# Keys and queries of the native jobs in one tile on space that w_out takes later; the limits loaded first; a shorter start of the first table

## The chip, the cores and the metric

The kernel runs on one core of one Trainium2 chip. The metric is the device time of one execution in microseconds, as the median of several runs. Where one execution was profiled, its own time stands beside its span, which is the part between the first and the last recorded instruction. The engines are named as the profile names them: PE multiplies matrices (PEld is its weight load), DVE, ACT and POOL work on tiles, SP issues DMAs.

## What is computed

The reference is attention with a local window and a few global keys, followed by a gated feed-forward part with a convolution along the sequence.

```python
B, H, S, D = 4, 8, 768, 64             # n_global 8, n_local 96
scores = q @ k.T / sqrt(D)             # per batch and head
keep   = key < n_global or 0 <= row - key < n_local
dist   = n_local for a global key outside the window, else |row - key|
scores = where(keep, scores - slope[head] * dist, -1e9)
a      = exp(scores - max); a = a / (sum(a) + 1e-9)
x      = (a @ v) laid out as (4, 768, 512)
h      = relu(x @ w_in)                # 512 -> 1024
c      = conv over 3 neighbours of the sequence with conv_w
out    = (h * sigmoid(c)) @ w_out      # 1024 -> 512
```

The limits n_global and n_local are inputs, so the table of distances and masks is built on the chip.

## The kernel before

**Work.** Attention is cut into 32 jobs: a batch, a half of the sequence (384 rows, `TB`), a pair of heads. A job has three steps of 128 rows, 96 steps in all. A step runs through the engines like this: scores on PE (`scores`, L620 for a native job, L622 and L623 for the others), the addition of the table and the maximum on DVE (`maximum`, L631, shown as CUSTOM_DVE or ISA), exponentials on ACT (L644), their sum and reciprocal on DVE (L654, L658), two normalisations on DVE, POOL or ACT (L667, L664), transposes on PE (L676, L677) and their way out of PSUM on ACT (`evict`, tile `pt`, L683). After three steps PE multiplies with the values (`pv`, L693), ACT and DVE split the result in a high and a low part (`xh` L707, `xl` L712), and PE can use it in `h` products (L725, three per block of 128, each 384 columns). The second half of the feed-forward part, `o` products, is L818.

**Native jobs.** The first nine jobs (`NATIVE`) multiply queries and keys as they are, in fp32. The others load keys and queries twice over (`rk`, `rq`), ACT or POOL casts them (`kk`, `qh`; L356), and DVE subtracts to get the low part (`split_k`, L360; `split_q`). Before the change the native jobs use the same buffers as these, `rk` and `kk` for keys, `qh` and `ql` for queries, with three loads for a job: keys of a whole pair of heads and two halves of queries. So `rk` of job 9 cannot be loaded before the native jobs are through with it.

**Weights.** w_in and w_out are 64-bit numbers and come in 16 pieces of 512 columns: a load `wr` (SP, L545), then ACT (`weight_top`, L552), DVE (`weight_bits`, L557), a cast on POOL (`weight_high`, L562) and a subtraction on DVE (`weight_low`, L568). Eight pieces make w_in, eight w_out.

**The table.** DVE computes `num` from the limits `nn` (L426), then `edge` (L431), which ACT needs for two operations on `off` (`beyond`, L457 and L458). The operation on the last eight columns of `off` (L461, in `middle`) waits for these two and stands in DVE's queue ahead of the first maximum.

**Order.** A planner (`Plan`) puts every instruction of the main part in order on each engine when the kernel is built. It has a cost, a due time and a list of needs for each, and times at which the engines are taken to start (`started`). Each engine works through its own list strictly as it stands. Where the planner sees PE waiting in the first 40 us it puts fillers (`warm`, L382), small products that nobody reads. SP issues nearly all loads in one queue.

Of the kernel before, what the change touches and what calls it, by code (L numbers as in the profile page):

```python
# [10 lines left out]
F32 = mybir.dt.float32  # L11
# [20 lines left out]
W0 = P  # L32
# [12 lines left out]
QROW = (0, 1, 2, 3, 0, 1, 2, 3, 2)  # L45
HK = 1024
# [232 lines left out]
WAIT = {"PE": 0, "ACT": 0, "DVE": 0, "POOL": 0, "SP": 0}  # L279
GAIN = {"PE": 0, "ACT": 0, "DVE": 0, "POOL": 0, "SP": 0}  # L280
LOADS = ("ldk", "ldq", "ldv", "wl", "lcw", "cl", "out")
# [12 lines left out]
def fast_path(tc, io):  # L294
# [24 lines left out]
    def zero_q(m):  # L319
        t = raw[m, "q"] = p2.tile([P, 2 * TB], F32, tag="qh" if m % 2 else "ql", name=f"rq{m}")  # L320
        G.memset(t[:D, TB:], 0.0)
        G.memset(t[D:, :TB], 0.0)

    def load_k(m):
        b, u, hp = jobs[m]
        w = NKC[u]
        if m < NATIVE:
            if m % 2 == 0:
                X, tag = (p2, "kk") if m // 2 % 3 else (p1, "rk")
                raw["pair"] = X.tile([P, HK], F32, tag=tag, name=f"rk{m}")  # L330
            c = m % 2 * (HK // 2)
            t = raw[m, "k"] = raw["pair"][:, c : c + w]
            nc.sync.dma_start(t, io["kn%d" % u][b, hp])
        else:
            t = raw[m, "k"] = p1.tile([P, 2 * w], F32, tag="rk", name=f"rk{m}")
            nc.sync.dma_start(t, io["qk%d" % u][b, hp][:, 2 * TB :])

    def load_q(m, j):
        b, u, hp = jobs[m]
        if m < NATIVE:  # L340
            r = slice(D * j, D * j + D)
            E = nc.sync if m + j else nc.scalar
            t = raw[m, "q"] = raw[QROW[m], "q"]
            E.dma_start(t[r, j * TB : j * TB + TB], io["qn"][b, hp, r, u * TB : u * TB + TB])
        else:
            t = raw[m, "q"] = p1.tile([P, 2 * TB], F32, tag="rq", name=f"rq{m}")
            nc.sync.dma_start(t, io["qk%d" % u][b, hp][:, : 2 * TB])
# [28 lines left out]
    nc.scalar.dma_start(nn, io["nn"].bitcast(I32).partition_broadcast(P))  # L376
# [40 lines left out]
    lt = pg.tile([P, NT], F32, tag="gh", name="lt")  # L417
# [5 lines left out]
    V.scalar_tensor_tensor(rel[:, gW], lt[:, gW], FAR, rel[:, gW], ALU.mult, ALU.add)  # L423
    nv = nn.rearrange("p (a b) -> p a b", a=2)
# [5 lines left out]
    edge = const.tile([P, 2], F32, name="edge")  # L430
    V.tensor_scalar(edge, wrap, nl, None, ALU.subtract)  # L431
# [78 lines left out]
    wih = const.tile([P, NK, FF], F32R, name="wih")  # L510
    wil = const.tile([P, NK, FF], F32R, name="wil")
    woh = const.tile([P, NF, DM], F32R, name="woh")
    wol = const.tile([P, NF, DM], F32R, name="wol")
# [10 lines left out]
    def weight_planes(i):  # L524
        if i < NK:
            h, l = wih[:, i], wil[:, i]
        else:
            j = i - NK
            h = woh[:, 2 * j : 2 * j + 2].rearrange("p f d -> p (f d)")
            l = wol[:, 2 * j : 2 * j + 2].rearrange("p f d -> p (f d)")  # L530
        return (x.rearrange("p (f n) -> p f n", f=NF) for x in (h, l))

    wraw, wt = {}, {}

    HW = HF * P

# [22 lines left out]
    def weight_high(i, half):  # L559
        t = wt[i, half]  # L560
        h, l = weight_planes(i)
        G.tensor_copy(h[:, half * HF : (half + 1) * HF], t)  # L562

    def weight_low(i, half, eng="DVE"):
        t = wt[i, half]
        h, l = weight_planes(i)
# [42 lines left out]
    def scores(s, j):  # L609
# [9 lines left out]
        if m < NATIVE:  # L619
            T.matmul(o, raw[m, "q"][:, qs], raw[m, "k"][:, k0 : k0 + n], start=True, stop=True)  # L620
            return
# [671 lines left out]
```

## Time and profile before

| what | value |
|---|---|
| median of three runs | 417.99 us (417.34 to 418.04) |
| the profiled execution | 416.73 us, its span 414.9 us |
| PE busy | 406.1 us, 98% of the span |
| DVE busy | 354.0 us, 85% |
| ACT busy | 321.2 us, 77% |
| POOL busy | 102.7 us, 25% |
| granted clock of PE | 0.998 of full speed |

The profiled execution has 1.83 us outside the span and lies 1.26 us below the median. A busy engine is one that has an instruction under way; these are means over the whole span, and the stretches differ: the first 40 us hold the loads of the weights and the first jobs, then PE hardly pauses.

### The profile page before, as it was taken

How to read it: one execution, taken by the hardware profiler on the slowest of the kernel's cores; microseconds unless marked ns; L12 is line 12 of the kernel's file. 1: busy time of each engine (PE TensorE's matmuls, PEld its weight loads, DVE VectorE, ACT ScalarE, POOL GpSimd, SP SyncE). 2: the span in 40 equal slices, each digit the busy share in tenths (PEclk: the TensorE clock that was granted, in tenths of full speed). 3: DMA queues.
4: the chain of work that ended last, by engine and by line, in shares of the span. 5: the costliest groups of instructions: out<-in, count | busy, mean ns of one | idle time of the engine just before them, and what ended most of it. 6: DMA issues, size and time to landing. Idle time of an engine off the chain costs nothing.

```text
span 414.9 us, 8589 instructions
## 1 busy us (share of the span) xinstructions
PE 406.1 (98%) x2895; PEld 365.6 (88%) x2895; DVE 354.0 (85%) x1039; ACT 321.2 (77%) x832; POOL 102.7 (25%) x161
## 2 busy tenths in 40 slices
PE   8899999999999999999999999999999999999996
PEld 7778998998899878999899888999899988898885
DVE  7989999999999999899998888699998986586700
ACT  5988999997899878798889876599788966276301
POOL 7322444643301412231223100042223200001000
PEclk9999999999999999999999999999999999999999
DMA  7999644443441334435351334534343154990111
GB/s 218 307 347 315 221 114 131 154 143 108 162 143 40 116 128 153 132 89 163 115 169 33 115 132 131 150 114 124 106 157 89 51 153 127 291 342 28 51 52 56
DMA packets 22513, 59.85 MB, mean 144 GB/s; under 512 B 2880, under 2 KB 5440, under 8 KB 22464
## 3 DMA queue, kind: packets, MB, share of 16 engines
q1 hardware_dynamic: 21952, 58.89, 44.5%
q8 instruction: 24, 0.39, 0.4%
q10 hardware_dynamic: 512, 0.36, 0.3%
q14 instruction: 25, 0.20, 0.2%
HBM read 52.95 MB, written 6.29 MB: 143 GB/s over the span
## 4 chain that ended last, share of the span: by engine, by line
PE 64%; DVE 15%; ACT 10%; DMA 6%; issue 2%; SPq 1%; ACTq 0%; DVEq 0%
PE o L818 26%; PE h L725 20%; PE pv L693 5%; DMA wr<-in_w 4%; PE t L677 3%; ACT pbuf L644 3%; PE s L623 3%; PE s L622 3%; DVE s L631 3%; PE t L676 2%; DVE c L758 2%; DVE kk L360 2%; DVE gl L808 2%; ACT pt L683 1%; PE e L846 1%
## 5 line engine op out<-in xcount | busy, mean ns | idle before, releaser
L725 PE MATMUL h<-xh,wih 128*128 128x384 f32 x256 | 92.1, 360 | 0.0
L644 ACT ACTIVATE pbuf<-s,mm 128x232 f32<-128x232 f32 (+1 forms) x192 | 83.2, 445 | 11.2 <-DVE mm L631 10.1
L725 PE MATMUL h<-xh,wil 128*128 128x384 f32 x256 | 86.4, 337 | 0.0
L725 PE MATMUL h<-xl,wih 128*128 128x384 f32 x256 | 86.3, 337 | 0.0
L758 DVE SCALAR_TENSOR_TENSOR c<-hbuf,cw,c 128x382 f32<-128x382 f32 (+1 forms) x128 | 79.1, 640 | 3.9 <-POOL c L756 3.3
L631 DVE CUSTOM_DVE_ANT_0 s<-s,tab 128x232 f32<-128x232 f32 (+1 forms) x192 | 73.0, 381 | 4.8 <-PE s L623 2.9
L818 PE MATMUL o<-woh,gh 128*128 128x512 f32 x184 | 74.9, 407 | 0.0
L818 PE MATMUL o<-woh,gl 128*128 128x512 f32 x184 | 72.7, 395 | 0.0
L818 PE MATMUL o<-wol,gh 128*128 128x512 f32 x184 | 72.6, 395 | 0.0
L683 ACT ACTIVATE pt<-t 128x464 f32<-128x464 f32 (+1 forms) x96 | 51.4, 535 | 10.4 <-PE t L677 9.6
L667 POOL TENSOR_SCALAR pbuf<-pbuf,mm 128x232 f32<-128x232 f32 (+1 forms) x44 | 32.3, 734 | 96.2 <-DVE mm L658 63.9
L725 PEld LDWEIGHTS h<-xh,wih 128*128 128x128 f32 x256 | 48.3, 189 | 0.2
L725 PEld LDWEIGHTS h<-xl,wih 128*128 128x128 f32 x256 | 48.3, 189 | 0.2
L725 PEld LDWEIGHTS h<-xh,wil 128*128 128x128 f32 x256 | 48.0, 188 | 0.0
L756 POOL TENSOR_SCALAR c<-hbuf,cw 128x382 f32<-128x382 f32 (+1 forms) x34 | 25.4, 752 | 89.5 <-ACT hbuf L733 80.4
L677 PE MATMUL t<-eye,pbuf 128*128 128x128 f32 x192 | 45.3, 276 | 0.1
L667 DVE TENSOR_SCALAR pbuf<-pbuf,mm 128x232 f32<-128x232 f32 (+1 forms) x115 | 42.5, 390 | 1.1
L818 PEld LDWEIGHTS o<-woh,gl 128*128 128x128 f32 x184 | 34.6, 188 | 8.2
L693 PEld LDWEIGHTS pv<-pt,v 128*64 128x64 f32 (+1 forms) x704 | 35.9, 136 | 6.3 <-issue 4.2
L644 ACT ACTIVATION_READ_ACCUMULATOR pbuf<-s,mm 128x1 f32 x192 | 40.4, 210 | 0.0
L693 PE MATMUL pv<-pt,v 128*64 128x128 f32 (+1 forms) x704 | 39.9, 266 | 0.5 <-ACT pt L683 0.5
L818 PEld LDWEIGHTS o<-woh,gh 128*128 128x128 f32 x184 | 34.7, 189 | 5.6
(116 smaller groups left out, 816.0 us busy)
## 6 DMA issues: line engine op xcount, KB each, us to landing
v<-in_vv SPq DMA_DIRECT2D x32, 384.0 KB, 3.7
rq<-in_qk SPq DMA_DIRECT2D x23, 384.0 KB, 3.6
check<-in_w SPq DMA_DIRECT2D x16, 512.0 KB, 4.1
wr<-in_w SPq DMA_DIRECT2D x16, 511.6 KB, 6.3
rk<-in_qk SPq DMA_DIRECT2D x12, 504.0 KB, 3.9
out<-ob SPq DMA_DIRECT2D x23, 256.0 KB, 2.2
rk<-in_qk SPq DMA_DIRECT2D x11, 400.0 KB, 3.3
rq<-in_qn SPq DMA_DIRECT2D x17, 96.0 KB, 5.6
```

The costliest lines, as they stand in the source:

```text
L622: T.matmul(o, qk[m, "h"][:, qs], qk[m, "k"][:, ks], start=True, stop=False)
L623: T.matmul(o, qk[m, "l"][:, qs], qk[m, "k"][:, ks], start=False, stop=True)
L631: V.tensor_tensor_reduce(out=o, in0=o, in1=tab[:, h, WIN:] if first else tab[:, h, 0:WIN], scale=-0.125, scalar=3.0e38, op0=ALU.add, op1=A ...
L644: last_exp[s] = A.activation(weights_of(s, j), st_s[s][:, j, :n], AF.Exp, bias=mm[:, j : j + 1], scale=-1.0, accum_out=mm[:, 2 + 2 * j : 3 ...
L667: X.tensor_scalar(x, x, y, 1.0, ALU.mult, ALU.mult)
L677: T.transpose(pt[:, c : c + P], pb[:, c : c + P], turned)
L683: A.activation(sb[:, :, :n], pt[:, :, :n], AF.Copy)
L693: T.matmul(pv[m][64 * j : 64 * j + 64, i * P + q : (i + 1) * P], vt[m][:n, i, c, 64 * j : 64 * j + 64], sb[:n, j, c * P : c * P + P - q], ...
L725: T.matmul(ps[:, :TB], w_[:, k, f * P : (f + 1) * P], x_, start=part == 0 and k == 0, stop=part == 2 and k == NK - 1,)
L756: G.tensor_scalar(c, h, x, 1.0, ALU.mult, ALU.mult)
L758: V.scalar_tensor_tensor(c, h, x, c, ALU.mult, ALU.add)
L818: T.matmul(ps, g_[:, f], w_[:, f], start=f == 0 and part == 0, stop=f == NF - 1 and part == 2,)
```

## The change

Keys and queries of a native job go to one of four tiles (`slots`, 1160 columns), whose space is that of the planes 2 to 7 of w_out (`plane`). The upper 64 partitions hold the first head and the lower 64 the second, each half in one load (`na`, `nb`): two loads for a job in place of three. The planes that lie there are written only after the last scores of the last job that used the slot (`lent`). The native jobs no longer hold `rk`, `kk`, `qh` and `ql`.

The limits `nn` move from ACT's first DMA to SP's first. In the table, two scaled copies of `rel` (`part`) are made before `num`, so that `table_w` is an operation on eight columns and one on 128; `wide` does later what the first table did before; `edge` stands behind two operations on `off`. Some of the planner's numbers change too.

```diff
-    nc.scalar.dma_start(nn, io["nn"].bitcast(I32).partition_broadcast(P))
+    nc.sync.dma_start(nn, io["nn"].bitcast(I32).partition_broadcast(P))
...
+    wof = [const.tile([P, 2, DM], F32R, name=f"wo{t}") for t in range(2)]
+    slots = [p1.tile([P, 3 * DM], F32, tag=f"wo{x}", name=f"slot{x}")[:, :NAT] for x in range(4)]
...
+    def load_n(m, j):
+        b, u, hp = jobs[m]
+        t = slots[SLOT[m]]
+        raw[m, "k"] = t[:, TB + KW - NKC[u] : TB + KW]
+        raw[m, "q"] = [t[:, TB + KW :], t[:, :TB]]
+        E = nc.sync if m + j else nc.scalar
+        if j == 0:
+            E.dma_start(t[:D, TB + KW - NKC[u] :], io["na%d" % u][b, hp])
+        else:
+            E.dma_start(t[D:, : TB + KW], io["nb%d" % u][b, hp])
...
+    for h in range(2):
+        V.tensor_scalar(part[h], rel[:, W], -(2.0 ** (2 - h)), 1.0, ALU.mult, ALU.mult)
...
-    edge = const.tile([P, 2], F32, name="edge")
-    V.tensor_scalar(edge, wrap, nl, None, ALU.subtract)
...
+    def table_w(h):
+        x = -(2.0 ** (2 - h))
+        V.tensor_scalar(part[h][:, :NGLOB], rel[:, gW], nl, x, ALU.min, ALU.mult)
+        V.scalar_tensor_tensor(tab[:, h, W], off[:, W], x * FAR, part[h], ALU.mult, ALU.add)
+
+    def wide():
+        V.tensor_scalar(rel[:, gW], rel[:, gW], nl, None, ALU.min)
+        masked(W)
+
     outside(W)
-    V.tensor_scalar(rel[:, gW], rel[:, gW], nl, None, ALU.min)
     V.scalar_tensor_tensor(off[:, gW], keyf, ng, off[:, gW], ALU.is_ge, ALU.min)
-    masked(W)
-    table(0, W)
-
+    edge = const.tile([P, 2], F32, name="edge")
+    V.tensor_scalar(edge, wrap, nl, None, ALU.subtract)
+    table_w(0)
...
+    def lent(p, t):
...
+        f = 2 * (p[0] - NK) + p[1]
+        x = 2 * t + (f - 2) // 3
+        return [("s", NB * m + NB - 1, 1) for m in range(NATIVE) if f >= 2 and SLOT[m] == x and x not in SLOT[m + 1 :]]
...
-    started = dict(PE=5000.0, ACT=1200.0, DVE=5200.0, POOL=7000.0, SP=700.0, DMA=1500.0)
...
+    started = dict(PE=4000.0, ACT=750.0, DVE=4500.0, POOL=7000.0, SP=1200.0, DMA=1800.0)
```

**DVE, from the limits to the first maximum.** Before, the list reads like this (`num` are the limits as numbers, `setup` holds `rel`, ISA is the maximum):

```order
L426 SCALAR_TENSOR_TENSOR num<-nn 128x2
L431 TENSOR_SCALAR edge<-wrap,num 128x2
L443 SCALAR_TENSOR_TENSOR off<-setup,num,lt 128x128
L449 TENSOR_SCALAR setup<-setup,num 128x8
L450 SCALAR_TENSOR_TENSOR off<-keyf,num,off 128x8
L446 SCALAR_TENSOR_TENSOR setup<-off,setup 128x128
L440 TENSOR_SCALAR tab<-setup 128x128
L454 TENSOR_SCALAR setup<-keyf,num 128x8
L461 TENSOR_SCALAR off<-keyf,num 128x8
L446 SCALAR_TENSOR_TENSOR setup<-off,setup 128x232
L631 ISA s_217,mm_185<-s_217,tab 128x128
```

With the change there is this in its place; the line numbers are those of the changed kernel:

```order
L436 TENSOR_SCALAR lt<-setup 128x128 x2
L439 SCALAR_TENSOR_TENSOR num<-nn 128x2
L454 SCALAR_TENSOR_TENSOR off<-setup,num,lt 128x128
L469 SCALAR_TENSOR_TENSOR off<-keyf,num,off 128x8
L471 TENSOR_SCALAR edge<-wrap,num 128x2
L461 TENSOR_SCALAR lt<-setup,num 128x8
L462 SCALAR_TENSOR_TENSOR tab<-off,lt 128x128
L473 TENSOR_SCALAR setup<-keyf,num 128x8
L480 TENSOR_SCALAR off<-keyf,num 128x8
L457 SCALAR_TENSOR_TENSOR setup<-off,setup 128x232
L638 ISA s_213,mm_188<-s_213,tab 128x128
```

`edge` has moved from directly behind `num` to behind two operations on `off`, the mask of 128 columns has left this stretch, and two scaled copies (into `lt`) stand ahead of `num`. The operation on eight columns of `off` that waits for ACT (L480, before L461) is still two places ahead of the first maximum.

**POOL, after the tables.** Before, POOL casts pieces of weights (`wih`) with normalisations (`pbuf`) between them:

```order
L562 CAST wih<-w_0_380 128x512
L562 CAST wih<-w_0_387 128x512
L667 TENSOR_SCALAR pbuf_182<-pbuf_182,mm_185 128x128
L562 CAST wih<-w_0_422 128x512
L562 CAST wih<-w_0_468 128x512
L667 TENSOR_SCALAR pbuf_182<-pbuf_182,mm_188 128x128
L562 CAST wih<-w_1_531 128x512
L562 CAST wih<-w_1_541 128x512
```

With the change the key cast of job 9 (`kk`) comes as the third of these:

```order
L570 CAST wih<-w_0_396 128x512
L674 TENSOR_SCALAR pbuf_185<-pbuf_185,mm_188 128x128
L366 CAST kk_463<-rk_340 128x800
L570 CAST wih<-w_0_443 128x512
L674 TENSOR_SCALAR pbuf_186<-pbuf_186,mm_189 128x232
L674 TENSOR_SCALAR pbuf_187<-pbuf_187,mm_190 128x232
L570 CAST wih<-w_0_505 128x512
L570 CAST wih<-w_0_534 128x512
```

A second key cast, that of job 10, follows this piece directly. Behind the first one stand the cast of the second weight piece and two normalisations, of steps 7 and 8.

**DVE, around the second `xl`.** Before, three operations on weight pieces lie near it:

```order
L654 TENSOR_REDUCE mm_186<-mm_186 128x2
L557 SCALAR_TENSOR_TENSOR w_0_422<-wr_0_276,w_0_422 128x512
L658 RECIPROCAL mm_186<-mm_186 128x2
L557 SCALAR_TENSOR_TENSOR w_0_468<-wr_0_347,w_0_468 128x512
L667 TENSOR_SCALAR pbuf_183<-pbuf_183,mm_186 128x232
L712 TENSOR_TENSOR xl_502<-pv_454,xh_490 128x384
L654 TENSOR_REDUCE mm_187<-mm_187 128x2
L631 ISA s_477,mm_188<-s_477,tab 128x128
```

With the change the first key split follows `xl` and a reciprocal (`mm`):

```order
L661 TENSOR_REDUCE mm_189<-mm_189 128x2
L638 ISA s_434,mm_190<-s_434,tab 128x232
L638 ISA mm_190 128x1
L719 TENSOR_TENSOR xl_484<-pv_446,xh_472 128x384
L665 RECIPROCAL mm_189<-mm_189 128x2
L370 TENSOR_TENSOR kk_463<-rk_340,kk_463 64x800
L574 TENSOR_TENSOR wil<-w_0_443,wih 128x512
L638 ISA s_498,mm_191<-s_498,tab 128x128
L638 ISA mm_191 128x1
```

The split has come in ahead of the subtraction for the second weight piece, which is the row behind it, and of the maxima of step 9. Of the weight pieces' operations DVE has fewer up to here. A second key split stands ahead of the third `xl`; before, the first key split stands behind the subtraction of the ninth weight piece.

On SP the key load of job 9 is the nineteenth DMA with the change, behind the loads of jobs 0 to 5, two loads of values and four weight pieces. On ACT a piece's `weight_top` comes some steps later in the list than before: the first four stand behind the evictions of steps 3 and 5, exponentials of step 8 and those of step 9, where before the first two stand behind the exponentials of step 5, the others behind the eviction of step 4 and the exponentials of step 7. On PE the program has 114 fillers in place of 85, of which 36 stand at the very start in both. Ahead of the transposes of step 14 stand nine `h` products fewer than before.

## Rows read from the trace of the kernel before

**Rows 1.** Busy time by stretch; columns as in its first line.
```profile
core 0: us, PE busy (x) PEld busy (x) DVE busy (x) ACT busy (x) POOL busy (x), PEclk, DMA share, GB/s
5.00:40.00 35.00, 32.57 (x278) 28.29 (x279) 32.99 (x145) 28.98 (x95) 11.94 (x25) 1.00 0.98 322
75.00:400.00 325.00, 324.45 (x2238) 292.42 (x2237) 283.96 (x761) 254.25 (x638) 70.46 (x86) 1.00 0.40 126
```

**Rows 2.** Waits of PE from 5 to 40 us: total, times, longest.
```profile
PE t L676 <- ACT pt L683: 1.2, 3, 0.8
PE pv L693 <- ACT pt L683: 0.5, 1, 0.5
PE s L620 <- ACT pbuf L644: 0.4, 1, 0.4
```

**Rows 3.** Waits of ACT in the same stretch.
```profile
ACT w L552 <- DMA wr<-in_w: 3.0, 4, 1.1
```

**Rows 4.** Waits of DVE in the same stretch.
```profile
DVE w L557 <- ACT w L552: 0.4, 1, 0.4
DVE xl L712 <- ACT xh L707: 0.3, 1, 0.3
```

**Rows 5.** Timeline of DVE, 2.5 to 6.5 us: start, duration, instruction, idle before.
```profile
2.52 0.41 DVE L419 TENSOR_SCALAR lt<-setup 128x128 f32<-128x128 f32 x1
...
3.77 0.16 DVE L426 SCALAR_TENSOR_TENSOR num<-nn 128x2 f32<-128x2 int32 x1 [0.64 <-DMA nn<-in_nn]
3.96 0.23 DVE L431 TENSOR_SCALAR edge<-wrap,num 128x2 f32<-128x2 f32 x1
4.10 0.35 DVE L443 SCALAR_TENSOR_TENSOR off<-setup,num,lt 128x128 f32<-128x128 f32 x1
...
4.88 0.29 DVE L446 SCALAR_TENSOR_TENSOR setup<-off,setup 128x128 f32<-128x128 f32 x1
...
5.48 0.38 DVE L461 TENSOR_SCALAR off<-keyf,num 128x8 f32<-128x8 f32 x1
...
6.22 0.29 DVE L631 CUSTOM_DVE_ANT_0 s<-s,tab 128x128 f32<-128x128 f32 x1
```

**Rows 6.** Timeline of ACT: the second of the two operations on `off`.
```profile
4.75 0.49 ACT L458 ACTIVATE off<-off,edge 128x232 f32<-128x232 f32 x1
```

**Rows 7.** Timeline of SP: a load of values, which ends a run of issues.
```profile
5.34 0.58 SPq L352 DMA_DIRECT2D v<-in_vv  x1
```

**Rows 8.** Busy time and rate of the DMA engines, 21.5 to 27.1 us.
```profile
21.50:27.10 5.60, 5.19 (x34) 4.72 (x34) 4.91 (x21) 4.61 (x15) 1.28 (x2) 1.00 0.98 330
```

**Rows 9.** Timeline of ACT: a weight piece taken up as it lands.
```profile
21.48 0.78 ACT L552 ACTIVATE w<-wr,misc 128x512 uint32<-128x512 fp8e4 x1 [0.90 <-DMA wr<-in_w]
```

**Rows 10.** Timeline of POOL: a key cast.
```profile
66.88 0.85 POOL L356 CAST kk<-rk 128x800 fp32r<-128x800 f32 x1 [0.66 <-DMA rk<-in_qk]
```

**Rows 11.** Timeline of DVE around the second `xl`.
```profile
21.12 0.68 DVE L557 SCALAR_TENSOR_TENSOR w<-wr,w 128x512 uint32<-128x512 uint32 x1
...
23.53 0.56 DVE L712 TENSOR_TENSOR xl<-pv,xh 128x384 fp32r<-128x384 f32 x1 [0.26 <-ACT xh L707]
```

**Rows 12.** Timeline of DVE: a key split.
```profile
70.09 0.99 DVE L360 TENSOR_TENSOR kk<-rk,kk 64x800 fp32r<-64x800 f32 x1
```

**Rows 13.** Timeline of DVE: the reciprocal of step 14.
```profile
39.48 0.16 DVE L658 RECIPROCAL mm<-mm 128x2 f32<-128x2 f32 x1
```

**Rows 14.** Timeline of POOL: one of the two normalisations behind it.
```profile
40.19 0.62 POOL L667 TENSOR_SCALAR pbuf<-pbuf,mm 128x232 f32<-128x232 f32 x1 [1.75 <-PE t L677]
```

**Rows 15.** Timeline of PE: step 14's first transpose.
```profile
42.73 0.25 PE L676 MATMUL t<-eye,pbuf 104*104 104x104 f32 x1
```

**Rows 16.** Chain of waits: a run of `h` products on PE.
```profile
167.99 2.61 PE h L725 x15
```

**Rows 17.** Timeline of PE: a run of fillers.
```profile
27.26 0.61 PE L382 MATMUL h<-setup 128*128 128x128 bf16 x8
```

**Rows 18.** Timeline of PE: its two waits between 40 and 160 us.
```profile
73.19 0.38 PE L622 MATMUL s<-kk,qh 128*128 128x232 f32 x1 [0.38 <-ACT pbuf L644]
...
148.41 0.27 PE L676 MATMUL t<-eye,pbuf 104*104 104x104 f32 x1 [0.49 <-ACT pbuf L664]
```

More of the change, by code (lines that the diff above doesn't have):

```diff
@@ L278 @@
 MORE = {("t", "PE"): 0, ("pv", "PE"): 0, ("nrm", "POOL"): 78, ("nrm", "ACT"): 46, ("exp", "ACT"): 45}
-WAIT = {"PE": 0, "ACT": 0, "DVE": 0, "POOL": 0, "SP": 0}
+WAIT = {"PE": 0, "ACT": 1, "DVE": 0, "POOL": 0, "SP": 0}
 GAIN = {"PE": 0, "ACT": 0, "DVE": 0, "POOL": 0, "SP": 0}
-LOADS = ("ldk", "ldq", "ldv", "wl", "lcw", "cl", "out")
+LOADS = ("ldn", "ldk", "ldq", "ldv", "wl", "lcw", "cl", "out")
 WARMEND = 40000.0
@@ new lines, in plane, with zero_q @@
+    def plane(t, f):
+        if f < 2:
+            return wof[t][:, f]
+        g, i = divmod(f - 2, 3)
+        if (t, g) not in wog:
+            wog[t, g] = p1.tile([P, 3, DM], F32R, tag=f"wo{2 * t + g}", name=f"wo{t}{g}")
+        return wog[t, g][:, i]
+    def zero_q(x):
+        G.memset(slots[x][D:, TB + KW :], 0.0)
+        G.memset(slots[x][:D, :TB], 0.0)
+    def load_n(m, j):
[8 more added lines that the diff above has]
+            E.dma_start(t[D:, : TB + KW], io["nb%d" % u][b, hp])
@@ L415, in fast_path @@
     V.tensor_copy(keyf, keyi)
-    lt = pg.tile([P, NT], F32, tag="gh", name="lt")
+    lt = pg.tile([P, NT + 2 * W0], F32, tag="gh", name="lt")
+    part = [lt[:, NT + h * W0 :][:, :W0] for h in range(2)]
     W, M = slice(WIN, NT), slice(0, WIN)
@@ L522, in fast_path, with weight_plane @@
     zero_q(3)
[L524 to L531, printed above, removed]
+    def weight_plane(t, i, half):
+        x = (wih, wil)[t][:, i, half * HW : (half + 1) * HW] if i < NK else plane(t, 2 * (i - NK) + half)
+        return x.rearrange("p (f n) -> p f n", f=HF)
+    HW = HF * P
     wraw, wt = {}, {}
-    HW = HF * P
     def weight_words(i, half):
@@ L560, in weight_high @@
         t = wt[i, half]
-        h, l = weight_planes(i)
-        G.tensor_copy(h[:, half * HF : (half + 1) * HF], t)
+        G.tensor_copy(weight_plane(0, i, half), t)
     def weight_low(i, half, eng="DVE"):
-        t = wt[i, half]
-        h, l = weight_planes(i)
-        sl = slice(half * HF, (half + 1) * HF)
-        (V if eng == "DVE" else G).tensor_tensor(l[:, sl], t, h[:, sl].bitcast(F32), ALU.subtract)
+        h, l = (weight_plane(x, i, half) for x in range(2))
+        (V if eng == "DVE" else G).tensor_tensor(l, wt[i, half], h.bitcast(F32), ALU.subtract)
     words, seen = {}, []
@@ L619, in scores @@
         if m < NATIVE:
-            T.matmul(o, raw[m, "q"][:, qs], raw[m, "k"][:, k0 : k0 + n], start=True, stop=True)
+            q = raw[m, "q"][j][:, i * P : (i + 1) * P]
+            T.matmul(o, q, raw[m, "k"][:, k0 : k0 + n], start=True, stop=True)
             return
@@ L816, in mm2 @@
         ps = hist["o", b, t]
-        for part, (g_, w_) in enumerate(((gh, woh), (gh, wol), (gl, woh))):
+        for part, (g_, w_) in enumerate(((gh, 0), (gh, 1), (gl, 0))):
             T.matmul(
-                ps, g_[:, f], w_[:, f],
+                ps, g_[:, f], plane(w_, f),
                 start=f == 0 and part == 0, stop=f == NF - 1 and part == 2,
@@ L1145, in general @@
             decode(t[..., 0], t[..., 1], e, y)
-            h, l = weight_planes(i)
-            A.activation(h, w, AF.Copy)
-            G.tensor_tensor(l, w, h.bitcast(F32), ALU.subtract)
+            for half in range(2):
+                h, l = (weight_plane(t, i, half) for t in range(2))
+                x = w[:, half * HF : (half + 1) * HF]
+                A.activation(h, x, AF.Copy)
+                G.tensor_tensor(l, x, h.bitcast(F32), ALU.subtract)
         r0i = gp.tile([P, S], I32, tag="q", name="r0i")
```

80 lines of the change are left out of this document (31 added, 49 removed).

## The prediction

> **What bounds the kernel now.** I read the times by stretch first. From 75 us to 400 us PE is busy for 324.45 of 325 us; from 5 to 40 us it is busy for 32.57 of 35 us and runs fillers in part of that, DVE is busy for 32.99, and the DMA engines have a share of 0.98 [rows 1]. So the kernel ends when PE has done its work, plus whatever PE lost, and nearly all of the loss is made in the first 40 us. There DVE, with 2.0 us idle, sets the pace: it adds the table for every step and decodes the weights as well. Next come the waits of that stretch. PE waits 1.2 + 0.5 + 0.4 = 2.1 us for ACT [rows 2]. ACT in turn is held four times, 3.0 us in all, by a weight piece that has not landed [rows 3]; evictions and exponentials stand behind it. DVE loses 0.4 + 0.3 = 0.7 us to ACT in the same way [rows 4]. Later there are few waits: two between 40 and 160 us, of 0.38 and 0.49 us [rows 18].
>
> PE's order is fixed, so a late step is not made up by work that stands behind it. What counts is when a step's weights are ready, against how much useful work PE has in front of it.
>
> **The start.** DVE waits 0.64 us for the limits, which ends with `num` at 3.77 [rows 5]. The two scaled copies, 128 columns each like the operation of 0.41 us at 2.52 [rows 5], fit into that wait. With `nn` as SP's first DMA I put `num` at 3.6 (3.45 to 3.85). But `edge` now comes behind `num` (0.19 to the next start), `off` (0.35) and an eight-column operation: 3.6 + 0.19 + 0.38 + 0.15 = 4.3, where it was 3.96 [rows 5]. From the start of `edge` to the end of ACT's second operation there were 4.75 + 0.49 - 3.96 = 1.28 us [rows 5, 6], so ACT ends at 5.6 in place of 5.24, and the operation that waits for it, before at 5.48, starts at about 5.7. The mask of 128 columns (0.29) that left DVE's stretch buys nothing, since DVE stands waiting for ACT. The first maximum moves from 6.22 to about 6.5: **+0.3** (+0.15 to +0.55). Behind the waiting operation stand the mask of 232 columns and all maxima.
>
> **DVE's further work before step 14.** Counting the order of both up to the reciprocal of step 14: two key splits come in, 0.99 each [rows 12], +2.0; two operations on eight columns and three on the convolution's weights at about 0.15 (the spacing of the small ones in [rows 5]), +0.7; the mask of `wide` and one more table of 360 columns at about 0.3 each (0.29 for 128 columns [rows 5]), +0.6. One bits and one low operation of a weight piece go, 0.68 long [rows 11], 0.6 in pace, -1.2; three normalisations go to other engines, about -0.75. Sum **+1.4** (+1.2 to +1.7).
>
> **The holds of ACT.** With the weights taken up some steps later in ACT's list, the pieces have landed by then. DVE gets back the 0.7 us: **-0.7** (-0.7 to 0). DVE's other idle time, 2.0 - 0.7 = 1.3 us, is spread over short waits for scores and sums; an engine that runs later finds half of that done: **-0.6** (-1.0 to 0).
>
> **The keys of job 9.** They are now SP's nineteenth DMA. Up to their end the queue carries 5.91 MB: four jobs of 0.428, two of 0.455, two loads of values of 0.393, four weight pieces of 0.524 and 0.410 of keys. In before the queue's fourth weight piece ends at 21.48, where ACT takes it up [rows 9], and by the list it has 4.94 MB up to there. The next 5.6 us ran at 330 GB/s [rows 8]: 0.97 MB more take 2.9 us, which gives 24.4. Two issues fewer stand ahead of the first load of values, at 0.58 each [rows 7], so all comes up to 1.15 us sooner: 23.25. A cast on POOL takes 0.85 [rows 10], and the split can start at 24.1. When does DVE get to it? The second `xl` started at 23.53 and took about 0.5 [rows 11]. Up to there DVE has 0.8 less work (two bits operations and one low, against the copies and the eight-column ones), gets back the 0.7, and carries the +0.3: with the reciprocal it is through at 22.9. It is held **1.2 us** (0 to 2.5). All of step 9's maxima stand behind the split, and on POOL the normalisations of steps 7 and 8 behind the cast.
>
> [...]
>
> **To PE.** Sum on DVE at step 14: 0.3 + 1.4 - 0.7 - 0.6 + 1.2 = +1.6. In before the reciprocal of step 14 starts at 39.48 [rows 13] and its last normalisation ends at 40.19 + 0.62 = 40.81 [rows 14], while PE comes to the transposes at 42.73 [rows 15]: 1.9 us to spare. But PE has nine `h` products fewer ahead of them, 9 x 2.61/15 = 1.57 us [rows 16]. So 0.3 is left, and PE loses 1.6 - 0.3 = **+1.3** (-0.3 to +2.6). Step 15 has more to spare. The fillers, 29 more at 0.61/8 = 0.076 us [rows 17] or 2.2 us, stand where PE waits anyway; the loss to 40 us has room for them, so I cost them at nothing, and at up to 2.2 where PE should be on time.
>
> **Later.** The waits of 0.38 us at 73 and 0.49 us at 148 us [rows 18], with the gaps beside them, come from ACT and DVE being late in their lists, the one at 73 just as DVE does the first key splits (the split of [rows 12] starts at 70.09). Splits done early and some 2 us less of work in ACT's list up to step 24 relieve these: **-1.0** (-1.4 to 0). The planes of w_out that must wait for the slots come late: decoding them moves behind the native jobs, to where DVE is as full as before; I cost this at nothing, since PE has `h` products of the first block to do, and it is a loss of a us or more if an `o` product waits for a plane.
>
> **Sum.** +1.3 - 1.0 = +0.3: 417.0 for an execution like the profiled one (416.73). The median is 1.26 above it, so 418.3.
>
> **The rivals.** *Faster:* the keys land by 22.0, so DVE is not held. Then 0.3 + 1.4 - 0.7 - 0.6 = 0.4 on DVE, within 0.1 of what PE has to spare, and later -1.4: 416.7. For it: the first loads begin sooner and the start of the DMA queue had room. Against it: 5.91 MB by then is more than the list of before had landed. If, besides, PE's 2.1 us behind ACT [rows 2] are what paced that stretch, and not DVE, about 1 us more is given back: 415.7.
>
> *Slower:* the engines' bytes and not SP's issues set the early landings, so that the 1.15 us do not come. The keys land at 24.4, the split can start at 25.25, DVE is held 2.35 us, and with it POOL: 0.3 + 1.4 - 0.7 - 0.6 + 2.35 - 0.3 - 1.0 = +1.45, 419.4. It decides from a landing at about 23.8 on, each us later being one us. [...] Without the later gain it is 420.4.
>
> *The change does not do what it says:* the keys of job 9 and 10 come early, but the splits only trade places with the weights, step 14 keeps its spare time, and the waits at 73 and 148 return in other places. About 418.0.
>
> **How the numbers follow.** A measurement of this kernel can tell about 0.2%, 0.84 us, from no change. My forecast of 418.3 and the last rival lie within that; I give them 0.31 and 0.05. The faster rival gets 0.31, the slower 0.33, as the price of the held split is the least certain term and each of its two sides is as near. The range of 415.7 to 420.4 spans both; the forecast's own is 417.5 to 419.1.
>
> **What would show it.** In the profile after: `edge` at about 4.3 and the first maximum at 6.4 to 6.6; no wait of ACT for `wr`; a wait of POOL for the DMA `rk` near 22 to 24 us and behind it one of DVE's split for POOL of about 1 us; PE waiting for the transposes of step 13 or 14; no wait of PE at 73. The forecast is wrong if DVE's split does not wait, if PE loses over 1 us after 75 us because an `o` product waits for a plane of w_out, or if the fillers delay scores that were ready.

## The result and the profile after

The changed kernel takes 422.26 us (422.01 to 424.08, four runs), against 417.66 us for the kernel before in runs on the same chip. The ratio is 1.0125, with a 95% interval of 1.0089 to 1.0162: slower by about 4.6 us, and above the range of the prediction. (One correction to the text ahead: a slot is 384 + 504 + 384 = 1272 columns wide, not 1160.)

The profiled execution is the longest of the four, 424.08 us at a granted clock of 0.994 over its span; the other three ran at 0.999 to 1.000 and took 422.01 to 422.40. A likely cause of that difference of 1.9 us comes out below.

Busy time by stretch, in the columns of [rows 1]:

```profile
5.00:40.00 35.00, 29.08 (x246) 25.43 (x247) 28.33 (x124) 24.43 (x78) 10.60 (x23) 0.95 1.00 287
75.00:400.00 325.00, 323.57 (x2262) 291.51 (x2262) 289.36 (x783) 260.80 (x655) 76.12 (x92) 1.00 0.41 129
```

In the first stretch PE, DVE and ACT each do less than in [rows 1]: DVE 28.33 of 35 us in place of 32.99. The DMA engines are as busy as before, 1.00 to 0.98, and move less, 287 to 322 GB/s. PE's granted clock has a mean of 0.95. From 75 to 400 us PE is busy for 323.57 us, 0.9 less than before. So the loss is made early again. It is larger than the idle time says, since fillers count as busy: those behind 20 us take 2.6 us (26 of them), against 0.9 (11) before. Who waits there, from 5 to 40 us (total, times, longest), first PE, then DVE, then POOL:

```profile
PE t L683 <- POOL pbuf L674: 4.2, 1, 4.2
PE s L627 <- POOL slot L335: 1.0, 1, 1.0
PE t L683 <- ACT pt L690: 0.5, 1, 0.5
PE t L683 <- DVE pbuf L674: 0.4, 1, 0.4
```

```profile
DVE kk L370 <- POOL kk L366: 4.5, 1, 4.5
```

```profile
POOL kk L366 <- DMA rk<-in_qk: 6.4, 1, 6.4
```

These answer to [rows 2 to 4]. PE's waits for evictions have shrunk from 1.2 to 0.5 us and ACT is no longer held by `wr` at all (no such row is left), as forecast. PE's 1.0 us is the wait for its first scores, at 5.69. In place of the others stands one long wait on each engine, and they make a chain: POOL 6.4 us for the DMA of `rk`, DVE 4.5 us for POOL's `kk`, PE 4.2 us for POOL's normalisation. (POOL also waits 9.8 us for weight pieces, ahead of this and behind it.) In the order of time, from the timelines of POOL, DVE and PE:

```profile
26.09 0.85 POOL L366 CAST kk<-rk 128x800 fp32r<-128x800 f32 x1 [6.42 <-DMA rk<-in_qk]
26.89 0.62 POOL L570 CAST wih<-w 128x512 fp32r<-128x512 f32 x1
27.48 1.19 POOL L674 TENSOR_SCALAR pbuf<-pbuf,mm 128x232 f32<-128x232 f32 x1
```

```profile
22.31 0.16 DVE L665 RECIPROCAL mm<-mm 128x2 f32<-128x2 f32 x1
26.98 1.36 DVE L370 TENSOR_TENSOR kk<-rk,kk 64x800 fp32r<-64x800 f32 x1 [4.51 <-POOL kk L366]
```

```profile
23.89 0.66 PE L627 MATMUL s<-slot 128*128 128x232 f32 x2
28.73 0.42 PE L683 MATMUL t<-eye,pbuf 104*104 104x104 f32 x1 [4.18 <-POOL pbuf L674]
```

POOL has its next instruction, the key cast of job 9, in hand from 19.7 on and starts it at 26.09. Behind it in its list stand a weight piece and, at 27.48, the normalisation of step 7. DVE is through with what stands ahead of the split at 22.47 and starts it at 26.98. PE gets its transposes of step 7 at 28.73, after 4.18 us with nothing in hand. The split itself takes 1.36 us, with a cast on POOL beside it, where [rows 12] had 0.99; the normalisation that starts beside it takes 1.19, where [rows 14] had 0.62.

The start, on DVE, beside [rows 5]:

```profile
3.29 0.48 DVE L436 TENSOR_SCALAR lt<-setup 128x128 f32<-128x128 f32 x2
3.82 0.16 DVE L439 SCALAR_TENSOR_TENSOR num<-nn 128x2 f32<-128x2 int32 x1
4.02 0.35 DVE L454 SCALAR_TENSOR_TENSOR off<-setup,num,lt 128x128 f32<-128x128 f32 x1
...
4.55 0.31 DVE L471 TENSOR_SCALAR edge<-wrap,num 128x2 f32<-128x2 f32 x1
...
5.94 0.23 DVE L480 TENSOR_SCALAR off<-keyf,num 128x8 f32<-128x8 f32 x1 [0.33 <-ACT off L477]
...
6.52 0.29 DVE L638 CUSTOM_DVE_ANT_0 s<-s,tab 128x128 f32<-128x128 f32 x1
```

`num` comes at 3.82, where it was 3.77: as SP's first DMA the limits land no sooner here, at 3.80. (In a kernel without half loads, the last one below, `num` came at 3.59.) `edge` is at 4.55, the operation that waits for ACT at 5.94, and the first maximum at 6.52, 0.30 later than before.

### The profile page after: what moved, and what is told of

The parts are those of the page before. It is cut to its first block, busy times and chain, and to the rows that moved or that the text cites. A ratio compares the mean times of both kernels' runs of the same rounds, so it can differ in the third digit from the quotient of the medians.

```text
span 422.3 us, 8640 instructions
## 1 busy us (share of the span) xinstructions
PE 409.7 (97%) x2924; PEld 368.4 (87%) x2924; DVE 355.3 (84%) x1040; ACT 322.5 (76%) x834; POOL 106.0 (25%) x162
## 4 chain that ended last, share of the span: by engine, by line
PE 69%; DVE 20%; issue 4%; ACT 4%; POOL 1%; DMA 1%; DVEq 0%; POOLq 0%; ACTq 0%
PE o L825 25%; PE h L732 23%; PE pv L700 6%; DVE s L638 4%; PE t L684 3%; DVE c L765 3%; PE t L683 3%; PE s L630 3%; PE s L629 2%; PE s L627 2%; DVE pbuf L674 2%; DVE gl L815 2%; DVE kk L370 1%; PE e L853 1%; ACT pbuf L651 1%
## 5 line engine op out<-in xcount | busy, mean ns | idle before, releaser
L825 PE MATMUL o<-wo,gh 128*128 128x512 f32 x368 | 117.5, 400 | 0.0
L765 DVE SCALAR_TENSOR_TENSOR c<-hbuf,cw,c 128x382 f32<-128x382 f32 (+1 forms) x128 | 82.4, 669 | 2.7 <-POOL c L763 1.4
L825 PEld LDWEIGHTS o<-wo,gh 128*128 128x128 f32 x368 | 64.7, 189 | 10.4
L825 PE MATMUL o<-wo,gl 128*128 128x512 f32 x184 | 72.4, 394 | 0.0
L690 ACT ACTIVATE pt<-t 128x464 f32<-128x464 f32 (+1 forms) x96 | 50.4, 525 | 11.4 <-PE t L684 11.0
L674 POOL TENSOR_SCALAR pbuf<-pbuf,mm 128x232 f32<-128x232 f32 (+1 forms) x41 | 27.6, 674 | 94.9 <-DVE mm L665 45.5
L683 PE MATMUL t<-eye,pbuf 104*104 104x104 f32 x160 | 38.3, 261 | 6.5 <-POOL pbuf L674 4.2
L674 DVE TENSOR_SCALAR pbuf<-pbuf,mm 128x232 f32<-128x232 f32 (+1 forms) x111 | 40.8, 388 | 1.0
L825 PEld LDWEIGHTS o<-wo,gl 128*128 128x128 f32 x184 | 34.5, 188 | 7.9
L651 ACT ACTIVATION_READ_ACCUMULATOR pbuf<-s,mm 128x1 f32 x192 | 38.2, 199 | 0.0
```

Source lines behind the costliest of these rows:

```text
L651: last_exp[s] = A.activation(weights_of(s, j), st_s[s][:, j, :n], AF.Exp, bias=mm[:, j : j + 1], scale=-1.0, accum_out=mm[:, 2 + 2 * j : 3 ...
L674: X.tensor_scalar(x, x, y, 1.0, ALU.mult, ALU.mult)
L683: T.transpose(pt[:NLATE, c + P : c + WIN], pb[:NLATE, c + P : c + WIN], ident[:NLATE, :NLATE])
L690: A.activation(sb[:, :, :n], pt[:, :, :n], AF.Copy)
L765: V.scalar_tensor_tensor(c, h, x, c, ALU.mult, ALU.add)
L825: T.matmul(ps, g_[:, f], plane(w_, f), start=f == 0 and part == 0, stop=f == NF - 1 and part == 2,)
```

## The experiments

Two theories came out of this. **Held lists:** the cast and the split of job 9's keys stand in POOL's and DVE's lists at a place that comes up well before the keys land, and all that is behind them pays. **Slow halves:** the keys land late, later than any row of before suggests, because loads into 64 partitions move slowly. The rivals: it is just the bytes ahead in the queue; all loads and steps are late anyway and the hold only shows it; the start is what costs. All kernels are timed against the kernel before, whose median was between 416.89 and 417.66 us in the sets of runs. So the difference of two medians from different sets is open by up to 0.8 us; the ratio, with its 95% interval in brackets, is the better measure. Where a clock is named without a stretch, it is the mean over the span of a run.

### Keys over 128 partitions, order unchanged

```diff
-        if j == 0:
-            E.dma_start(t[:D, TB + KW - NKC[u] :], io["na%d" % u][b, hp])
-        else:
-            E.dma_start(t[D:, : TB + KW], io["nb%d" % u][b, hp])
+        if j:
+            nc.sync.dma_start(raw[m, "k"], io["kn%d" % u][b, hp])
+        r = slice(D * j, D * j + D)
+        E.dma_start(raw[m, "q"][j][r], io["qn%d" % u][b, hp, r])
...
```

> The changed kernel with the same order, but each native job's keys come in one load over all 128 partitions and the queries in two loads over 64, as before the change (into the new tiles). Theory 'slow halves': loads over 64 partitions with long rows move at about 240 GB/s where loads over 128 move at about 340, so job 9's keys land about 2 us sooner (24 in place of 26.0), DVE's split is held about 2.5 us in place of 4.5, and the time falls by about 2 us, to about 420.2. Rival 'too much ahead in the queue': the keys are late because of the bytes ahead of them, at whatever shape; then with one more issue per job they land at 26 or later and the time stays at 422 to 423.

The keys' cast and split in this kernel, on POOL and DVE:

```profile
24.25 0.85 POOL L366 CAST kk<-rk 128x800 fp32r<-128x800 f32 x1 [4.60 <-DMA rk<-in_qk]
```

```profile
25.14 1.36 DVE L370 TENSOR_TENSOR kk<-rk,kk 64x800 fp32r<-64x800 f32 x1 [2.69 <-POOL kk L366]
```

The keys come 1.84 us sooner (24.25 for the cast, from 26.09), with one issue more per job, and DVE is held 2.7 us in place of 4.5. That is what slow halves said and the rival did not. One trace each would not carry it, so here are all with this list of loads, by the DMA records: with halves the keys landed at 26.04, 25.87 and 26.35 us (the changed kernel and two below that have its loads), with whole keys at 24.20, 25.39 and 23.77 (this one and two below), 1.6 us sooner in the mean. The halves carry 0.11 MB more for the four jobs with a gap (0.428 MB each, against 0.401), 0.3 us at 330 GB/s, so the bytes ahead explain a small part. The rate says it too. Two stretches of the changed kernel and of this one (columns as in [rows 1]):

```profile
5.00:10.00 5.00, 4.31 (x25) 3.94 (x25) 4.37 (x25) 3.22 (x12) 2.40 (x10) 1.00 1.01 256
20.00:25.00 5.00, 4.54 (x40) 3.62 (x36) 2.44 (x10) 3.97 (x13) 0.00 (x0) 1.00 1.05 261
```

```profile
5.00:10.00 5.00, 4.65 (x25) 3.92 (x25) 4.41 (x24) 3.21 (x12) 2.40 (x10) 1.00 0.97 295
20.00:25.00 5.00, 4.52 (x40) 3.60 (x36) 2.42 (x10) 3.94 (x13) 0.75 (x1) 1.00 1.00 317
```

With halves the engines are busy for the whole stretch and move 256 and 261 GB/s; with whole keys 295 and 317. Worked out from the packets of the trace that began between 5 and 25 us, by size:

```
kernel      bytes  partitions  packets  mean us  16 engines at that pace
before       4093     128        755     0.179    366 GB/s   weights
before       3072     128        384     0.146    337 GB/s   values
before       1600     128        254     0.073    353 GB/s   keys
before       2016     128        310     0.096    337 GB/s   keys
before       1536      64        577     0.098    250 GB/s   queries
after        4093     128        526     0.198    331 GB/s   weights
after        3072     128        366     0.167    294 GB/s   values
after        3200     128        124     0.194    264 GB/s   keys of job 9
after        3552      64        439     0.236    240 GB/s   half loads
after        3136      64        134     0.222    226 GB/s   half loads
whole keys   4093     128        616     0.195    335 GB/s   weights
whole keys   1600     128        363     0.080    320 GB/s   keys
whole keys   2016     128        279     0.120    270 GB/s   keys
whole keys   1536      64        627     0.084    292 GB/s   queries
```

A half load moves at two thirds of the pace that keys and weights had before (226 to 240 GB/s, against 337 to 366). It is not the length of the rows, since the weights' are longer and faster (4093 bytes, 331 GB/s in the same kernel). But the number of partitions alone does not give the pace of a load either: beside half loads the keys of job 9, over 128 partitions, move at 264 GB/s, and with whole keys the short rows of the queries, over 64, are no slower (292) than the keys of 2016 bytes (270). What holds in every trace is the sum: in these two stretches the queue moves 250 to 262 GB/s in the four kernels with half loads of long rows and job 9's keys at this place. With whole keys and the same places it moves 295 and 317 in this kernel; the two others, below, had 303 and 338 from 20 to 25 us. The change put the native keys, which moved at 337 to 353 GB/s, into the slow kind. What makes a half load slow, no run here shows.

The time did not fall, however: 423.47 us (1.0146, 1.0114 to 1.0179), 3 us above what was expected. All four runs were at a clock of 0.992 to 0.996, where three of the changed kernel's four were at 0.999 or 1.000. That needed a run of its own.

### The same, with fillers in the hold

```diff
+        if o.key == ("t", 7, 1):
+            warm(32)
```

> The kernel with keys over 128 partitions in the order of the changed kernel, with 32 fillers ahead of the second pair of transposes of step 7, where PE is held 2.4 us. Theory 'the hold is paid twice': the granted clock falls to about 0.5 to 0.8 for 5 us behind the hold, in all four runs of that kernel (0.992 to 0.996 over the span), and that costs up to 2 us; with fillers the clock stays at 1.00 and the time falls from 423.5 to about 421.5. If the clock's fall costs nothing there, as DVE sets the pace: 423.5.

PE's clock around the hold, in the kernel without and with fillers (the clock is the third number from the end):

```profile
22.50:27.50 5.00, 2.64 (x17) 1.89 (x15) 2.33 (x5) 2.06 (x7) 2.57 (x3) 1.00 0.97 318
27.50:32.50 5.00, 5.00 (x30) 4.68 (x29) 3.85 (x19) 3.12 (x10) 1.31 (x2) 0.66 0.89 322
32.50:37.50 5.00, 4.46 (x45) 3.76 (x43) 4.90 (x15) 4.03 (x14) 1.41 (x2) 1.00 0.82 264
```

```profile
22.50:27.50 5.00, 3.80 (x44) 3.14 (x42) 1.18 (x1) 1.88 (x6) 2.06 (x3) 1.00 1.03 323
27.50:32.50 5.00, 4.24 (x33) 3.90 (x33) 4.92 (x21) 3.26 (x11) 1.83 (x3) 1.00 0.95 324
32.50:37.50 5.00, 4.29 (x41) 3.74 (x42) 4.90 (x15) 3.96 (x14) 1.41 (x2) 1.00 0.92 292
```

Without fillers the stretch from 27.5 to 32.5 us, behind the hold, ran at a mean of 0.66 (0.53 in its first half, 0.79 in its second); with 32 idle products in the hold it ran at 1.00. The time is 421.52 us, against 423.47, and the clock 0.998 to 1.000 in all five runs. By ratios it is 1.0093 (1.0059 to 1.0127) against 1.0146 (1.0114 to 1.0179). So the hold is paid twice: PE stands still, and then it works through these 5 us, busy for all of them, at a mean clock of 0.66, which by an estimate from that mean costs (1 - 0.66) x 5 = 1.7 us there. In the changed kernel this seems to fall on some executions and not on others. The profiled one had it: 0.66 in the same stretch, and 0.50 from 28.5 to 31.0 us, at 424.08 against 422.0 to 422.4; of the other three only the mean clock is known. (In the profile of the filled kernel the keys came at 25.4 and DVE was held 3.9 us, so the loads vary by a microsecond between executions.) Where the clock holds, whole keys are worth 422.2 - 421.5, about 0.7 us, which these runs do not tell from nothing.

### Cast and split later

```diff
+    for key, behind in ((("ck", 9), ("max", 11, 1)), (("sk", 9), ("max", 12, 1)), (("ldk", 10), ("sk", 9)), (("ck", 10), ("max", 16, 1)), (("sk", 10), ("max", 17, 1)), (("ldk", 11), ("sk", 10))):
+        x = next(d for d in done if d[1].key == key)
+        done.remove(x)
+        done.insert(next(i for i, d in enumerate(done) if d[1].key == behind) + 1, x)
```

> The changed kernel with all loads up to job 9's keys where they are, but the cast and the split of these keys moved behind the maxima of steps 11 and 12 on POOL and DVE, and the load, cast and split of job 10's (and the load of job 11's) moved behind accordingly. Theory 'held lists': what costs the time is that POOL and DVE stand waiting for a load with the work of steps 7 to 9 behind them; then DVE's hold of 4.5 us and PE's of 4.2 us go, and the time is 418 to 419. Rival 'everything comes later': the weights and jobs are late as well, and the hold only shows it; then PE's loss moves to other waits and the time stays above 421.

PE's waits over 0.2 us from 25 to 50 us, in the timeline:

```profile
35.48 0.27 PE L683 MATMUL t<-eye,pbuf 104*104 104x104 f32 x1 [1.10 <-DVE pbuf L674]
...
49.55 0.66 PE L627 MATMUL s<-slot 128*128 128x232 f32 x2 [1.02 <-ACT pbuf L651]
```

The hold is gone, on POOL (0.36 us are left of 6.42) and on PE; the two waits that remain in this stretch are 1.10 and 1.02 us. The time is 420.81 us (1.0091, 1.0060 to 1.0123). That is above the 418 to 419 expected. So the held list cost about 1.5 us, beside what it does to the clock (the intervals overlap), and both theories fall short: by the ratio 3.8 us are still there. A split moved by hand in a fixed order removes the wait; the rest of the order stays as it was made, for keys, weights and queries that land earlier than they do.

### Both edits

The diff of the whole keys and the one of the later cast and split together.

> Both of the edits that the runs before tried one at a time: keys of the native jobs in one load over 128 partitions, and cast and split of job 9's keys behind the maxima of steps 11 and 12. Theory 'slow halves and held lists', both costing: with the split moved, 3.5 us of loss are left over the kernel before, made between 30 and 50 us where loads are late; loads that move at the full rate take away about 2 us of that: 418.5 to 419. Rival 'one cause': the shape of the loads matters only through the keys of job 9; then nothing is gained over the 420.8 of the moved split alone.

420.03 us (1.0080, 1.0051 to 1.0109), above the 418.5 to 419 expected. That is 0.8 us below the moved split alone, with intervals that overlap, and 3 us remain. In this kernel neither the half loads of keys nor the hold is left; what is left is an order made from other landing times. The next runs change that.

### The planner told of the half loads' price

```diff
-                add(("ldn", m, j), ("SP" if m + j else "ACT", (dma(D, (TB + (KW if j else w)) * 4), 0)), (load_n, m, j), old, due=D0 - 8900 + j)
+                add(("ldn", m, j), ("SP" if m + j else "ACT", (1.6 * dma(D, (TB + (KW if j else w)) * 4), 0)), (load_n, m, j), old, due=D0 - 8900 + j)
```

> The changed kernel with the planner's price for each load over 64 partitions multiplied by 1.6, nothing else; the planner then puts the cast of job 9's keys behind one more weight piece on POOL and the split behind the maxima of step 10 on DVE, and other places follow. Theories 'slow halves' and 'held lists' together: DVE's hold falls to 2 to 3 us, and the time to about 420. If the order around the split doesn't matter: 422.

Nothing else in the program differs; the planner makes its whole order anew, with other fillers. 419.03 us (1.0035, 1.0012 to 1.0058), where 420 was expected. The split on DVE, now behind the maxima of step 10:

```profile
27.38 1.37 DVE L370 TENSOR_TENSOR kk<-rk,kk 64x800 fp32r<-64x800 f32 x1 [0.29 <-POOL kk L366]
```

It starts at 27.38, later than in the changed kernel, and is held 0.29 us in place of 4.51 (2 to 3 us were expected). The keys land at 26.06, no sooner than in the changed kernel, so it is the order that wins and not an earlier landing. This is 3.2 us of the 4.6 that the change lost, from one number: the planner prices a load by its rows and their length, which makes a half load as fast per byte as any other. How much of the 3.2 us is the split's place, and how much another place in the new order, this run does not tell.

### The planner told of three loads, keys over 128 partitions

```diff
+            add(("ldn", m, 2), ("SP", (dma(P, w * 4), 0)), (load_n, m, 2), old, due=D0 - 9000)
             for j in range(2):
-                add(("ldn", m, j), ("SP" if m + j else "ACT", (dma(D, (TB + (KW if j else w)) * 4), 0)), (load_n, m, j), old, due=D0 - 8900 + j)
+                add(("ldn", m, j), ("SP" if m + j else "ACT", (dma(D, TB * 4), 0)), (load_n, m, j), old, due=D0 - 8900 + j)
...
```

> Keys over 128 partitions again, with the planner told of three loads for a job and their prices as before the change, so that it makes its own order. Theory 'slow halves and held lists': the planner's times for these loads now fit, so the casts and splits stand where the keys have landed; no hold of DVE over 1 us, and 416 to 418.5. Rival 'early keys cost by themselves' (two splits of 1 us more on DVE before 40 us): 419 or more even then.

417.71 us (1.0017, 0.9994 to 1.0040). No loss is left that these runs can tell from none, with the new tiles, the early keys and the new start all kept; the two loads for a job are given up. The kernel with both edits by hand has loads of the same shapes, and the intervals are apart (1.0051 to 1.0109 there). On DVE the split starts at 32.04 and waits for nothing:

```profile
32.04 1.09 DVE L371 TENSOR_TENSOR kk<-rk,kk 64x800 fp32r<-64x800 f32 x1
```

### Early keys, old place

Both with the load of job 9's keys not ahead of the last native scores, once in the changed kernel and once with whole keys and the planner told.

```diff
-            add(("ldk", m), ("SP", (dma(P, w * 8), 0)), (load_k, m), alloc=(bk,), due=D0 - 9000)
+            add(("ldk", m), ("SP", (dma(P, w * 8), 0)), (load_k, m), alloc=(bk,), due=D0 - 9000, behind=[("s", NB * NATIVE - 1, 1)])
```

> The changed kernel with the load of job 9's keys not before the last scores of a native job, as before the change; halves, limits and table as changed, order by the planner. Theory 'held lists' (the early keys are the larger part): 417.5 to 419. Rival 'slow halves' as the larger part: the native jobs' loads are as slow as in the changed kernel, so weights and later jobs land late and the time stays above 420.

419.69 us (1.0068, 1.0044 to 1.0093). Taking the early keys out of the changed kernel gives back 2.6 us, and 2 us stay. The halves are still there and may be what keeps them, which this run does not show. So neither theory holds it all.

> The same kernel of three loads for a job, with the load of job 9's keys not before the last native scores. Theory 'early keys are neither good nor bad once they are in time': 417 to 418.5. Rival 'early splits cost by themselves' (1 us of DVE before 40 us for each): below 417.0, faster than with early keys. Rival 'early keys pay' by closing the waits near 73 us: 418.5 or more.

418.42 us (1.0039, 1.0019 to 1.0060), with runs from 416.92 to 421.02; five of its twelve were at a clock of 0.994 to 0.996, and these five are the ones above 419.8. Not faster without early keys, so no cost of the early splits by themselves shows once they are in time; whether they pay is inside the scatter of the clock.

### The start

```diff
     nl, ng = num[:, 0:1], num[:, 1:2]
+    edge = const.tile([P, 2], F32, name="edge")
+    V.tensor_scalar(edge, wrap, nl, None, ALU.subtract)
...
-    edge = const.tile([P, 2], F32, name="edge")
-    V.tensor_scalar(edge, wrap, nl, None, ALU.subtract)
```

> The changed kernel with edge computed directly behind num again. Theory 'held lists': the first maximum moves from 6.52 to about 6.3, but the landing of job 9's keys sets the pace later, so the time stays at 422.2 within 0.3 us. Rival 'late start': the 0.3 us at the start goes through to the end, with what the steps behind it lose, and the time falls by 0.3 to 1 us.

423.56 us (1.0135, 1.0097 to 1.0174), with two runs at 424.1 and 424.3 and clocks of 0.996 and 0.995. DVE around the first maximum:

```profile
3.85 0.16 DVE L439 SCALAR_TENSOR_TENSOR num<-nn 128x2 f32<-128x2 int32 x1
4.05 0.35 DVE L444 TENSOR_SCALAR edge<-wrap,num 128x2 f32<-128x2 f32 x1
...
5.52 0.22 DVE L480 TENSOR_SCALAR off<-keyf,num 128x8 f32<-128x8 f32 x1
5.78 0.40 DVE L459 SCALAR_TENSOR_TENSOR setup<-off,setup 128x232 f32<-128x232 f32 x1
6.51 0.30 DVE L638 CUSTOM_DVE_ANT_0 s<-s,tab 128x128 f32<-128x128 f32 x1 [0.33 <-PE s L627]
```

`edge` is 0.5 us sooner and the operation behind ACT (L480) no longer waits. But the first maximum stays at 6.51, where 6.3 was expected, since it now waits 0.33 us for scores, and PE's first scores wait 0.8 us for a half load (`nb`). One wait took the place of another, and the time did not fall. It lies 1.3 us above the 422.2 expected, for which the two runs at a lower clock are the likely reason: the other two took 422.2 and 423.0.

The same edit in the kernel with whole keys and the planner told of three loads:

> The kernel with keys over 128 partitions and the planner told of three loads, with edge directly behind num. With halves this edit moved nothing, since the first maximum then waited for scores whose half load landed late; here the first job's loads land by 5.1, so the first maximum should come at 6.3 in place of 6.5, and the time fall by 0 to 0.3 us, to about 417.5. If it falls by 1 us or more, the start is worth more than its own delay.

417.06 us (0.9999, 0.9981 to 1.0018), 0.65 us below the same kernel without the edit, with intervals that overlap; the lowest median here, and level with the kernel before. The first maximum came at 6.56, 0.26 later than expected, against 7.04 without the edit; in both the planner put a table of 232 columns ahead of it.

In that kernel, without the edit, the start taken back to that of before:

```diff
-    nc.sync.dma_start(nn, io["nn"].bitcast(I32).partition_broadcast(P))
+    nc.scalar.dma_start(nn, io["nn"].bitcast(I32).partition_broadcast(P))
...
-    table_w(0)
+    masked(W)
+    table(0, W)
...
```

> The same kernel of three loads for a job in the new tiles, with the whole start (limits on ACT's queue, table, edge) as before the change. Theory 'the start costs little': within 0.8 us of 417.7, the sign open, since DVE has about 0.5 us less to do and the limits no later. Rival 'the new start pays': 418.5 or more.

417.33 us (1.0012, 0.9996 to 1.0029), level with 417.71 and 417.06: the new start shows neither a gain nor a cost. DVE's first maximum in this kernel:

```profile
7.51 0.28 DVE L630 CUSTOM_DVE_ANT_0 s<-s,tab 128x128 f32<-128x128 f32 x1
```

It is a microsecond later than in the changed kernel (6.52), and the time is 5 us lower. So the rival that the late start is what costs is out.

And the new start alone, in the kernel before, which is the reverse of that diff:

> The kernel before with only the changed start: limits as SP's first DMA, the two scaled copies, the shorter first table, edge behind two operations on off, wide later; loads of the native jobs as before the change, the rest by the planner with its numbers of before. Theory 'the start costs little': num comes no sooner (the limits landed at 3.80 with the change, at 3.75 before), edge later, the first maximum 0.2 to 0.3 us later than 6.22, and the time within 0.8 us of the kernel before. Rival 'the start is a good part of the loss': over 418.5.

418.14 us (1.0034, 1.0014 to 1.0054). The first maximum came at 6.39, 0.17 later, where 0.2 to 0.3 was expected, and `num` at 3.59, sooner than the 3.77 of before and not as late as expected. The time is at the edge of the 0.8 us allowed, and its interval lies above no change. PE's longest wait in this kernel's first 75 us is one of 1.3 us for ACT's exponentials, in an order that the planner made anew. What the start costs alone was not told apart from that. So an order made anew may cost the better part of a microsecond by itself, which was not tried apart, and a difference of that size between two kernels with different orders is not put down to their edit.

## Why the prediction was wrong

**The step that failed** is the one on the keys of job 9: "the split can start at 24.1", DVE "held **1.2 us** (0 to 2.5)". The mechanism was right, down to the engines and the normalisations behind it; the landing was mis-sized. By the trace's DMA records the keys landed at 26.04, not at 23.25, the split started at 26.98, and DVE was held 4.5 us. The loads had been put at the pace of before, and 1.15 us taken off for two issues fewer. The pace was lower: from 15 to 25 us the changed kernel moved 271 GB/s where the one before moved 310, although its DMA engines had the higher share (1.04 and 0.92). With whole keys the keys landed 1.6 us sooner in the mean, so the halves are about that much of the 2.8, give or take the microsecond by which executions differ.

The 1.15 us came at first and did not last. The first values landed at 10.22 in place of 11.48, but the fourth weight piece at 23.43 in place of 21.46. With three loads for a job the first values landed as early (10.22 to 10.70 in three traces), so the saved issues are not shown to be what helped. SP issued the keys' load at 15.24, 10.8 us before it landed: there the engines and not SP set the landing, as the slower rival had it (24.4). That rival named the place and the sign, but its price too was made with the pace of before.

In the changed kernel the first six half loads landed one after another, 0.8 to 1.1 us apart, from 4.64 to 9.45 us. By the packets from 5 to 25 us half loads moved at 226 to 240 GB/s, where the keys before moved at 337 to 353 and the queries, half loads too, at 250.

**To PE** failed next. The hold was put into the sum at step 14, less what PE had to spare there. It was paid at step 7, at once and in full (4.18 us), because PE's list had nothing else to do ahead of those transposes; and it brought the clock down in some runs, for which there was no term at all (1.9 us where it falls). With the measured hold in place of 1.2 us and nothing for the later gain, the prediction's own sum would be 0.3 + 1.4 - 0.7 - 0.6 + 4.5 - 0.3 = +4.6, or 422.6. That this is near 422.26 is in part chance, as the path was another and the small terms were not measured.

**Later, -1.0,** did not come. The waits near 73 and 148 us are gone, as forecast, and others took their place: PE has 0.7 + 0.4 us of waits behind 45 us in the changed kernel; 40 to 75 us lost 0.4 less than before and 75 to 400 us 0.9 more. A planner that knows the price does not end these: PE's waits behind 40 us add up to 3.7 us with the price alone and to 3.0 with whole keys. What those kernels win they win early, where PE is idle for 1.9 and 1.6 us from 5 to 40 us in place of 5.9.

**What held.** The first maximum: +0.30, forecast +0.3. In part that is luck, since `num` was at 3.82 and not at 3.6, `edge` at 4.55 in place of 4.3 and the operation that waits for ACT at 5.94 in place of 5.7, and from there to the maximum it took 0.58 us and not the 0.74 of before. ACT's holds by `wr`: gone. The planes of w_out in the slots: no `o` product waits for a plane in the list of waits. The fillers, put at nothing: the kernel with whole keys and the planner told has more of them behind 20 us (30, 2.2 us) and no loss, so their number is not what costs. The small terms on DVE (+1.4, -0.7, -0.6) were not measured one by one; the hold covers them.

**Size by the runs.** Of 4.6 us, by medians: telling the planner the price of the half loads gives back 3.2, replacing the halves with its knowledge 4.5, moving the two operations alone 1.5, the shape alone about 0.7 at full clock, which is not clear of the noise. These overlap and are not terms of a sum. What stays open is how the remaining 2.3 us between the kernel with both edits by hand (420.03) and the one with a new plan (417.71) spread over its order, and why a half load is slow.

## What to carry to other kernels

Take the pace of a load from a row of the same shape in a queue of the same kind: an average over a stretch hides two kinds of load, and here the loads beside slow ones were slower too (264 to 331 GB/s over 128 partitions, against 337 to 366 before). Where a planner orders the work, tell it that price; here this gave back more (3.2 us) than moving the held operations by hand (1.5 us). Before a transfer moves up a queue, look at what stands behind its first user on every engine, and where the list of the engine that bounds the kernel has nothing else to do. Merging transfers saves issues; ask first whether the issues set the landings, or the DMA engines, as they did here for the keys of job 9 (issued at 15.24, landed at 26.04).

## What was not expected of the hardware

With a hold of PE of 2.4 us (whole keys) and of 4.2 us (the changed kernel) the mean granted clock from 27.5 to 32.5 us was 0.66 in the profiled executions; by the mean clock of their spans, 0.999 to 1.000, the three other executions of the changed kernel do not seem to have had it. With whole keys and 32 products of zeros in the hold it was 1.00. By the packets from 5 to 25 us half loads of rows of 3.1 and 3.6 KB moved at 226 to 240 GB/s, and the loads over 128 partitions beside them at 264 to 331, where loads over 128 had 337 to 366 before.
